# Another stored list of 102 shifts for the planner that orders an attention and feed-forward kernel

## The chip, the cores and the metric

The kernel runs on one core of a Trainium2 chip. The metric is device time in microseconds (us): the median of three runs of the kernel before is 573.95 us (573.7 to 574.1).

## What is computed

Local attention with a summary of the far keys, and behind it a feed-forward layer on the same tokens. Four batches, eight heads, 768 positions, 64 columns a head; the feed-forward layer has 3072 tokens, 512 columns and 2048 hidden units.

```python
k_sum = k.reshape(B, H, nb, block, D).max(axis=3)      # block 32, window 16
v_sum = v.reshape(B, H, nb, block, D).mean(axis=3)
scores_l = scale * np.matmul(q, k.transpose(0, 1, 3, 2))
mask_l = np.abs(pos[:, None] - pos[None, :]) < window
scores_s = scale * np.einsum('bhsd,bhnd->bhsn', q, k_sum) + np.log(block)
scores_all = np.concatenate([np.where(mask_l, scores_l, -1e9), scores_s], axis=-1)
a = softmax(scores_all)
x = np.matmul(a, np.concatenate([v, v_sum], axis=2))   # heads side by side: 3072 x 512
h = x @ w_in
g = h * (1.0 / (1.0 + np.exp(-h)))
out = g @ w_out
```

## The kernel before

The tokens are worked on in 12 chunks of 256 (chunk 0 to chunk 11). Each chunk needs the attention of two tiles of 128 positions, and then the feed-forward layer over 16 blocks of 128 hidden units, taken two at a time. The attention of later tiles is computed while the feed-forward layer of earlier chunks fills TensorE.

Chunk zero uses 32-bit matmuls (L915, L928) while the weights arrive. From chunk one on, weights and activations are split into a high and a low 16-bit half, and three products stand for one. Chunks one and two take the plain form (`job_f`: first matmuls L918, second matmuls L931); in the trace L918 runs from 85.0 to 173.8 us. From chunk three on (`FAST = 3`) the second matmul is done with seven products instead of eight (`job_fast`: L1006, L1046), which needs sums of the weights ("quads", made by `job_quad`: GpSimd at L986, VectorE at L991) and sums of the activations (GpSimd or VectorE at L1031).

The steps that the prediction speaks of, by line. ScalarE's L813 and VectorE's L814 read a finished attention tile out of a PSUM bank and write its high and its low half; the bank may take the next tile's L781 or L796 only when both are done. L871 makes the low half of a pair of weight blocks. L540 to L545 make the halves of q and k of a later tile, and L437 to L442 the scales of a batch. L505 and L507 are reductions over v, L411 one over k, and ScalarE's L413 and L431 take sums over k and q. Their inputs are loaded (L504, L410, L430, L539) into three staging buffers (`raw`), each of which has to be read before the next load into it starts. L1071 combines the four accumulator banks of a finished fast chunk into its output, which also frees those banks for the next chunk; L1129 does it for the end of the last chunk. L273 and L720, L722 belong to the softmax of batch zero, L944 and L947 to the activation of chunks zero to two.

The order is not written out by hand. Every step is an operation with a cost in ns on each engine that may do it, with its dependencies and a priority. `sweep` is a list scheduler: among the operations that are ready it takes the one that can start first, and among equals the one with the lower priority number, and it chooses the engine with it. `schedule` runs sweeps forward and backward for six rounds, keeps the best priorities, and then applies `MOVES`. Each entry of `MOVES` is (seed, start of a window, its length, size, block), in ns: `move` adds a random number of that size to the priority of the operations that the present order starts within the window, and sweeps again. The order after the last entry is the one that is issued, instruction by instruction, on every engine and on SyncE's DMA queue.

VectorE and GpSimd operations carry `port=("dve", "pool")` unless the call says otherwise, and the scheduler doesn't let two such operations run side by side.

```python
    def move(self, order, seed, at, span, size, block):
        rng, by = random.Random(seed), {}
        for i in sorted(o[2] for o in order if at <= o[0] < at + span):
            if i // block not in by:
                by[i // block] = rng.gauss(0, size)
            self.prio[i] += by[i // block]
        return self.sweep(self.prio, None, False)
```

Of the kernel before, what the change touches and what calls it, by code (L numbers as in the profile page):

```python
# [54 lines left out]
APART = 2  # L55
SOLO = [(0,), (1,)]
MOVES = (
# [26 lines left out]
)  # L84
NSUP = 2
FAST = 3
# [1210 lines left out]
```

## Time and profile before

| | us |
|---|---|
| median of three runs | 573.95 |
| the profiled execution | 573.44 |
| its span, first to last instruction | 571.7 |
| TensorE busy | 559.9 |
| VectorE busy | 482.2 |
| ScalarE busy | 388.0 |
| GpSimd busy | 195.8 |

Busy times are sums over the span. A "busy" TensorE is one with a matmul in its pipeline, whose end is modelled, so short pauses between matmuls don't show. DVE is VectorE, ACT ScalarE, POOL GpSimd, SP SyncE (which issues the DMAs), PE TensorE's matmuls and PEld its weight loads. L12 is line 12 of the kernel.

### The profile page before, as it was taken

The numbers are of one execution on the slowest core, as the hardware profiler recorded it, in microseconds if no ns is written. First come the engines' busy times: TensorE is split into PE (matmuls) and PEld (weight loads), VectorE is DVE, ScalarE is ACT, GpSimd is POOL, SyncE is SP. The second block draws the span as 40 slices with busy tenths as digits, with TensorE's granted clock in tenths as the row PEclk, the third lists the DMA queues.
The fourth block names the chain that finished last, engine by engine and source line by source line (L and its number), as shares of the span: only waits on it lengthen the run. The fifth ranks groups of instructions, "written<-read, shape, count | busy, mean of one in ns | idle before, by whom it ended". The sixth has DMA issues, their size and how long they took to land.

```text
span 571.7 us, 16049 instructions
## 1 busy us (share of the span) xinstructions
PE 559.9 (98%) x6426; PEld 455.6 (80%) x6426; DVE 482.2 (84%) x1159; ACT 388.0 (68%) x983; POOL 195.8 (34%) x292
## 2 busy tenths in 40 slices
PE   7999999989999999899999999999999999999996
PEld 3767657766666888788888888888888888888885
DVE  6999989989898886999988878998977978845655
ACT  4999989757867973667768865648767755533342
POOL 4302101561745542355433314252434333211110
PEclk9999999999999999999999999999999999999999
DMA  8999733333784679363673856544754239110101
GB/s 324 420 418 415 278 109 97 97 109 106 188 226 93 204 153 94 109 188 114 198 187 107 209 134 74 118 137 126 214 144 125 70 66 65 47 30 1 38 2 37
DMA packets 66737, 83.93 MB, mean 147 GB/s; under 512 B 44950, under 2 KB 45350, under 8 KB 64870
## 3 DMA queue, kind: packets, MB, share of 16 engines
q1 hardware_dynamic: 66662, 82.91, 52.4%
q8 instruction: 50, 0.82, 0.6%
q14 instruction: 25, 0.20, 0.1%
HBM read 61.60 MB, written 11.16 MB: 127 GB/s over the span
## 4 chain that ended last, share of the span: by engine, by line
PE 83%; DVE 7%; DMA 5%; ACT 3%; issue 1%; POOL 0%; SPq 0%; DVEq 0%; ACTq 0%
PE bank L1006 30%; PE bank L1046 25%; PE bank L931 6%; PE bank L918 6%; PE bank L915 5%; PE bank L928 4%; PE bank L796 2%; DVE wr L871 2%; PE bank L668 2%; DMA raw<-in_qF_dram 2%; DMA raw<-in_vR_dram 1%; PE bank L781 1%; DMA second<-in_qP_dram 1%; ACT e L707 1%; DMA raw<-in_qkT_dram 1%; DVE e L704 1%
## 5 line engine op out<-in xcount | busy, mean ns | idle before, releaser
L1006 PE MATMUL bank<-x,wr 128*128 128x256 f16 x1728 | 205.8, 273 | 0.0
L1031 POOL TENSOR_TENSOR wr<-wr 128x256 f32<-128x256 f32 (+1 forms) x172 | 122.5, 713 | 240.5 <-DVE wr L1022 127.4
L1006 PEld LDWEIGHTS <-wr 128*128 128x128 f16 x1728 | 167.8, 98 | 20.4
L1046 PE MATMUL bank<-wr 128*128 128x256 f16 x1491 | 179.9, 273 | 1.5 <-DVE raw L1071 1.5
L1046 PEld LDWEIGHTS <-wr 128*128 128x128 f16 x1491 | 144.6, 98 | 19.4 <-issue 1.7
L1021 ACT ACTIVATE wr<-bank,th 128x512 f32<-128x512 f32 x71 | 48.5, 683 | 54.2 <-PE bank L1006 53.9
L707 ACT ACTIVATE e<-e,mx 128x120 f32<-128x120 f32 x192 | 73.2, 383 | 8.1 <-DVE mx L704 8.0
L1022 DVE SCALAR_TENSOR_TENSOR wr<-wr,bank 128x512 f32<-128x512 f32 x71 | 48.5, 683 | 32.0 <-ACT wr L1021 31.7
L1033 ACT ACTIVATE wr<-wr 128x512 f16<-128x512 f32 x71 | 44.5, 626 | 35.4 <-POOL wr L1031 34.8
L1034 DVE SCALAR_TENSOR_TENSOR wr<-wr 128x512 f16<-128x512 f32 x71 | 49.7, 700 | 15.3 <-ACT wr L1033 15.1
L1026 ACT ACTIVATE wr<-wr 128x384 f16<-128x384 f32 x71 | 36.8, 519 | 36.8 <-DVE wr L1022 36.8
L1027 DVE SCALAR_TENSOR_TENSOR wr<-wr 128x384 f16<-128x384 f32 x71 | 45.5, 641 | 2.8 <-ACT wr L1026 2.6
L918 PE MATMUL bank<-x,wr 128*128 128x256 f16 x384 | 45.4, 273 | 0.0
L918 PEld LDWEIGHTS <-wr 128*128 128x128 f16 x384 | 37.2, 98 | 8.1 <-issue 0.6
L704 DVE CUSTOM_DVE_ANT_0 e<-bank,masks,qsc 128x120 f32<-128x120 f32 x144 | 41.7, 336 | 0.3 <-PE bank L668 0.3
L986 POOL TENSOR_TENSOR wr<-wr 128x256 f32<-128x256 f32 x32 | 30.9, 977 | 16.3 <-DVE wr L991 7.5
L707 ACT ACTIVATION_READ_ACCUMULATOR e<-e,mx 128x1 f32 x192 | 36.3, 189 | 0.0
L722 POOL TENSOR_SCALAR e<-e,sum 128x120 f32<-128x120 f32 x30 | 11.4, 395 | 65.3 <-DVE sum L715 31.7
L915 PEld LDWEIGHTS bank<-x,wr 128*128 128x128 f32 x144 | 24.8, 190 | 7.7 <-issue 4.2
L928 PE MATMUL bank<-wr,work 128*128 128x512 f32 x64 | 30.6, 596 | 0.0
L915 PE MATMUL bank<-x,wr 128*128 128x256 f32 (+1 forms) x144 | 30.6, 359 | 0.0
L760 DVE TENSOR_TENSOR first<-e,first 128x480 f16<-128x480 f32 x36 | 25.5, 714 | 0.1
(170 smaller groups left out, 788.4 us busy)
## 6 DMA issues: line engine op xcount, KB each, us to landing
wr<-in_w_dram SPq DMA_DIRECT2D x14, 1024.0 KB
raw<-in_qkT_dram SPq DMA_DIRECT2D x18, 576.0 KB
out_dram<-raw SPq DMA_DIRECT2D x23, 256.0 KB
first<-vd SPq DMA_DIRECT2D x30, 192.0 KB
raw<-in_kF_dram SPq DMA_DIRECT2D x12, 384.0 KB
raw<-in_qF_dram SPq DMA_DIRECT2D x9, 512.0 KB
raw<-in_vR_dram SPq DMA_DIRECT2D x12, 384.0 KB
raw<-in_vP_dram SPq DMA_DIRECT2D x9, 512.0 KB
```

Of the source, the lines that this page charges most:

```text
L704: plan.op({"dve": 262 if b else 206}, lambda e, i=i, j=j, et=et, mx=mx: nc.vector.tensor_tensor_reduce(out=et[:, i, :], in0=sc[j][:, i, :N ...
L707: plan.op({"act": 385}, lambda e, i=i, j=j, et=et, mx=mx: nc.scalar.activation(out=et[:, i, :], in_=et[:, i, :], func=AF.Exp, scale=-1.0, ...
L915: nc.tensor.matmul(out=o, lhsT=wi[:, ct * P:(ct + 1) * P], rhs=x0[:, ct, cs], start=(ct == 0), stop=(ct == NCT - 1))
L918: nc.tensor.matmul(out=o, lhsT=wip[:, part, ct * P:(ct + 1) * P], rhs=x[:, ct, :], start=(ct == 0 and q == 0), stop=(ct == NCT - 1 and q = ...
L928: nc.tensor.matmul(out=bank[ob[u]], lhsT=t[:, rows], rhs=wo, start=begins, stop=stops)
L1006: nc.tensor.matmul(out=h[:, at * CH:at * CH + CH], lhsT=wip[:, p, ct * P:(ct + 1) * P], rhs=x[:, ct, :], start=(ct == 0 and q == 0), stop= ...
L1021: plan.op({"act": 573}, lambda e: nc.scalar.activation(out=t, in_=h, func=AF.Tanh, scale=th[:, 0:1]), r=bk(k) + [("th", b % 2), "areas"], ...
L1022: plan.op({"dve": 604}, lambda e: nc.vector.scalar_tensor_tensor(out=t, in0=t, scalar=1.0, in1=h, op0=ALU.add, op1=ALU.mult), r=bk(k), w=t ...
L1027: plan.op({"dve": 470}, lambda e: nc.vector.scalar_tensor_tensor(out=ld, in0=src, scalar=SHRINK, in1=hd, op0=ALU.mult, op1=ALU.subtract), ...
L1031: plan.op({"pool": 135 + 290 * size, "dve": 213 if size == 1 else 459}, lambda e, o=o, x=x, y=y: eng[e].tensor_tensor(out=o, in0=x, in1=y, ...
L1034: plan.op({"dve": 610}, lambda e: nc.vector.scalar_tensor_tensor(out=ls, in0=sf, scalar=SHRINK, in1=hs, op0=ALU.mult, op1=ALU.subtract), r ...
L1046: nc.tensor.matmul(out=acc_of(c, m)[0], lhsT=x[:, left[m]], rhs=right[m](p), start=(opens and q == 0 and m in (1, 4, 2, 7)), stop=(closes ...
```

## The change

The tuple `MOVES` is replaced: 101 entries go and 102 come. The new list was chosen on a plan in which vector work takes longer in chunks one and two. Nothing else in the kernel changes: the costs, the dependencies, the rules of the scheduler and the list of operations are those of before.

```diff
 MOVES = (
-    (77065967, 539892, 8000, 2000, 1), (350253771, 327181, 20000, 200, 2), (631126651, 448333, 50000, 600, 1), (703916009, 173609, 8000, 2000, 1),
-    (908351244, 27961, 20000, 600, 2), (828492973, 176901, 20000, 200, 2), (387453712, 523354, 3000, 15000, 2), (975260573, 463713, 8000, 600, 1),
...
-    (720944112, 503864, 3000, 15000, 12),
+    (46148794, 194900, 8000, 6000, 2), (259609208, 234228, 3000, 600, 2), (429151876, 239758, 3000, 6000, 2), (548233728, 510331, 8000, 2000, 2),
+    (223928855, 486020, 50000, 600, 12), (821097478, 542829, 3000, 6000, 1), (942257997, 140504, 3000, 600, 12), (559197850, 325128, 3000, 15000, 1),
...
+    (674030052, 86227, 20000, 200, 1), (878329011, 29366, 20000, 200, 1),
 )
```

Sorted by the start of their windows, the old list has 5 entries that begin before 24 us, 20 from 24 to 86, 19 from 86 to 186, 8 from 186 to 240 and 49 after that; the new list has 3, 13, 17, 10 and 59.

## Rows read from the trace of the kernel before

**Rows 1.** The page: TensorE's busy time, and its granted clock in 40 slices.

```profile
PE 559.9 (98%) x6426; PEld 455.6 (80%) x6426; DVE 482.2 (84%) x1159; ACT 388.0 (68%) x983; POOL 195.8 (34%) x292
...
PEclk9999999999999999999999999999999999999999
```

**Rows 2.** Stretches: length; busy PE, PEld, DVE, ACT, POOL; clock, DMA share, GB/s.

```profile
0.00:25.00 25.00, 21.52 (x341) 13.00 (x342) 19.05 (x82) 16.95 (x61) 10.38 (x38) 1.00 0.94 364
...
80.00:100.00 20.00, 19.40 (x175) 12.79 (x174) 19.68 (x42) 19.38 (x40) 2.29 (x4) 1.00 0.25 74
100.00:120.00 20.00, 18.39 (x218) 13.16 (x217) 18.75 (x47) 13.98 (x39) 11.63 (x19) 1.00 0.27 71
120.00:186.00 66.00, 66.00 (x731) 44.99 (x728) 59.09 (x136) 48.20 (x116) 32.66 (x35) 1.00 0.60 157
...
230.00:240.00 10.00, 8.49 (x118) 7.33 (x116) 9.98 (x30) 7.22 (x26) 3.74 (x7) 1.00 0.19 62
240.00:545.00 305.00, 305.00 (x3784) 269.52 (x3783) 252.82 (x605) 193.23 (x505) 107.02 (x146) 1.00 0.47 114
545.00:571.70 26.70, 22.13 (x194) 18.74 (x192) 15.28 (x31) 8.56 (x16) 2.55 (x4) 1.00 0.06 21
```

**Rows 3.** Waits: engine, line <- releaser: us in total, times, longest.

```profile
DVE am L507 <- DMA raw<-in_vR_dram: 3.9, 2, 3.5
...
PE bank L781 <- DVE x L814: 1.6, 1, 1.6
PE bank L1046 <- DVE raw L1071: 1.5, 1, 1.5
...
PE bank L735 <- DVE third L273: 0.3, 1, 0.3
PE bank L931 <- DVE work L947: 0.3, 1, 0.3
```

**Rows 4.** Timeline of TensorE near 120 us: start, length, what, idle before.

```profile
119.71 1.15 PE L781 MATMUL bank<-third,v 120*64 120x64 f32 x32 [1.55 <-DVE x L814]
```

**Rows 5.** Timeline of VectorE, 110 to 120 us.

```profile
110.82 0.16 DVE L437 TENSOR_SCALAR qc<-qc 128x2 f32<-128x2 f32 x1
...
111.96 0.70 DVE L439 TENSOR_SCALAR qc<-qc 128x2 f32<-128x2 f32 x1
...
115.19 0.68 DVE L442 SCALAR_TENSOR_TENSOR qsc<-qsc 128x1 f32<-128x1 f32 x1
115.79 1.27 DVE L871 SCALAR_TENSOR_TENSOR wr<-wr,ws 128x1024 f16<-128x1024 f32 x1
116.99 0.74 DVE L542 SCALAR_TENSOR_TENSOR second<-raw,qsc,second 128x512 f16<-128x512 f32 x1
117.65 1.34 DVE L545 SCALAR_TENSOR_TENSOR second<-raw,qsc,second 128x640 f16<-128x640 f32 x1
118.91 0.74 DVE L814 SCALAR_TENSOR_TENSOR x<-bank,vsc,x 128x512 f16<-128x512 f32 x1
```

**Rows 6.** Timeline of ScalarE, 115 to 117 us.

```profile
115.49 0.69 ACT L813 ACTIVATE x<-bank,vsc 128x512 f16<-128x512 f32 x1
```

**Rows 7.** Timeline of GpSimd, 108 to 124 us.

```profile
111.90 0.73 POOL L986 TENSOR_TENSOR wr<-wr 128x256 f32<-128x256 f32 x1
...
117.14 3.12 POOL L986 TENSOR_TENSOR wr<-wr 128x256 f32<-128x256 f32 x3 [1.29 <-DVE wr L871]
```

**Rows 8.** Lines L986 and L545: ns min/median/max, first and last start in us.

```profile
L986 POOL TENSOR_TENSOR wr<-wr x32: 720/894/1786, 111.9 to 186.5; 128x256 f32<-128x256 f32 x32
...
L545 DVE SCALAR_TENSOR_TENSOR second<-raw,qsc,second x18: 869/884/1344, 117.6 to 459.1; 128x640 f16<-128x640 f32 x18
```

**Rows 9.** The chain of work that ended last, in order of time: start, us, what.

```profile
94.71 0.85 DVE am L507
...
218.33 7.22 DMA raw<-in_vR_dram
...
234.42 0.74 DVE raw L1071
```

46 rows, old and new, of the table MOVES are left out of this document.

## The prediction

> **What bounds the kernel now.** I read the page's engine table first, then busy time by stretch, then what TensorE waited for, and last the lines around its two long waits. TensorE is busy 559.9 of 571.7 us at a granted clock of 0.9 or more of full speed in every slice, 1.00 by stretch, the upper of its two levels (2.4 GHz) [rows 1, 2]. So the end is set by TensorE's work plus the moments in which it has none, and a change of order can win only those moments. The stretches show where they lie: 3.48 us before 25 us, 0.60 between 80 and 100, 1.61 between 100 and 120, 1.51 between 230 and 240, 4.57 after 545, and none in the other stretches [rows 2]. (Ends of matmuls are modelled, so these are lower bounds, good enough to place the waits.) The table of waits names the middle ones: 1.6 us for VectorE's L814, 1.5 us for VectorE's L1071, and 0.3 twice for L273 and L947 [rows 3]. All four wait for VectorE, and three of the four lie in the stretches from 80 to 120 us, in chunk one; the wait for L1071 belongs to the end of chunk three.
>
> The longest wait in detail: TensorE's L781 starts at 119.71 after 1.55 us of idleness [rows 4], because it overwrites the bank that L814 still reads. L814's other input, ScalarE's L813, ended at 115.49 + 0.69 = 116.18 [rows 6]. But L814 started only at 118.91: ahead of it in VectorE's queue stood L871 (115.79), L542 (116.99) and L545 (117.65) [rows 5]. And the vector work there is longer than elsewhere: L439 on two columns takes 0.70 us where its neighbour L437 of the same shape takes 0.16, L442 takes 0.68, and L545 takes 1.34 where its median is 0.884 [rows 5, 8]. The same moments hold GpSimd's L986: 0.73 us from 111.90, and three of them in 3.12 us from 117.14 [rows 7]. L439 ended at 112.66, L986 at 112.63. The excess of the three vector instructions is (0.70 - 0.16) + (0.68 - 0.16, L437 standing for its base) + (1.34 - 0.88) = 1.52 us, as long as the wait itself.
>
> **The change part by part.** Nothing computed is added or removed: 101 stored shifts go, 102 come, and every cost, rule and dependency of the planner stays. What moves is the order of instructions on each engine and, with it, on SyncE's DMA queue; any operation that has more than one engine to choose from may change engine too. The new order isn't in the trace of before, so its terms are read as idle time that can go or come.
>
> *The wait for L814.* A list that was kept because it does well when vector work is slow in chunks one and two has a reason to put L814, which TensorE needs at once, ahead of L542 and L545, which serve scores of a later tile. The price of that order can be read: in L542's place, right behind L871, it would start at 116.99 instead of 118.91, 1.92 us earlier, more than the 1.55 to be won [rows 4, 5]. Value taken: -1.55 us. Bounds: 0, if another vector step takes L814's place in front of TensorE, and -1.55 - 2 x 0.3 = -2.15, if the two short waits of the same chunk [rows 3] go with it. I take the value between, because the two short waits hang on a stretch where VectorE is busy 19.68 of 20 us [rows 2] and there is no room to go ahead in.
>
> *The wait for L1071.* It is outside the two chunks. VectorE sat idle for 3.5 us until a load of vR had landed, 7.22 us after its issue at 218.33, and L1071 was reached at 234.42 after the burst that had piled up [rows 3, 9]. A longer booking of vector work two chunks earlier neither brings this load forward nor empties the three staging buffers. Value taken: 0. Bounds: -1.51 (the whole idle time of that stretch [rows 2]) and, above, the price worked out for the slower rival, below.
>
> *The rest of chunks three to eleven.* TensorE has no idle time from 240 to 545 us while VectorE is busy 252.8 of 305 us [rows 2]: shifts there are covered by 52 us of vector slack. Value 0; where that cover is locally gone the cost is one vector step, 0.74 us for an L1071 [rows 9], and nothing is to be gained.
>
> *Start and end.* Of the shifts whose window begins before 24 us the old list has five and the new three, so the first loads may come in another order. TensorE's idle time bounds the gain, 3.48 us at the start and 4.57 us at the end [rows 2]; the nearest row for a loss is one load landing late, up to 7.22 us [rows 9]. I take 0 for both, since idle time there follows from the first loads and the last store, which no order of vector work removes.
>
> The profiled execution took 573.44 us. Sum: 573.44 - 1.55 + 0 + 0 + 0 = 571.89. The median of the runs, 573.95, stands 0.51 above it, so on the median's scale: **572.4 us**.
>
> *A rule weighed.* The coincidence of L986 with the stretched vector steps [rows 5, 7] has a rule beside it. The Trainium skill, page "SBUF — State Buffer", section "SBUF: two separate sides", says that VectorE and GpSimd share one pair of ports as an exclusive lock: whoever starts first keeps it for the whole instruction and the other stands still. The trace agrees with it in L439, which ends within 0.03 us of L986. By the rule the collisions don't vanish in another order, which speaks against the change and is the second rival below; by the forecast's sum 571.89 stands, by the rule alone 573.44.
>
> **The rivals.**
> 1. *The wait moves but stays as long.* GpSimd's 32 quad steps of L986 still run between about 112 and 187 us at a median of 0.894 us [rows 8], and VectorE is already busy 18.75 + 59.09 of the 86 us from 100 to 186 [rows 2]. Only 8.2 us are free for whatever the collisions cost, 1.52 us for three of them. Another order lets them fall on other vector steps, and if one of those feeds TensorE, 1.5 us come back there: 573.95 us. The same time results if the change doesn't do what it says: the planner that replays the shifts keeps its old costs, so the windows may catch other operations than those they were chosen on. For it: the shifts' costs and rules are untouched, and TensorE's waits come from coincidences of this size. Against it: in 120 to 186 us the same L986 cost TensorE nothing [rows 2].
> 2. *Both waits go.* Any other order around 218 to 234 may issue the load of vR earlier. Then 573.95 - 1.55 - 1.51 = 570.9 us. For it: the wait for L1071 hangs on a single late load. Against: nothing in the change aims there.
> 3. *Slower: vector work put off from chunks one and two lands in front of L1071.* Booked longer, the reductions that can wait (L507 at 94.71, for instance, 0.85 us of the chain in chunk one [rows 9]) are pushed later, to where they stand with their loads between 190 and 238 us. There TensorE already waits, so there is no cover left. One more load of vR with its two reductions in front of L1071 costs 2 x 0.85 = 1.7 us if it has landed, and 7.22 + 1.7 - 3.5 = 5.4 us if it has not, the 3.5 being the idle time that exists anyway [rows 3, 9]. Middle 3.6. With the gain in chunk one kept that is 573.95 - 1.55 + 3.6 = 576.0 us. It decides from 1.55 + 1.15 = 2.7 us of added delay, so from about 2.7 - 1.7 = 1.0 us of waiting for a load that is not there in time.
>
> **How the numbers follow.** A measurement of this kernel can tell about 0.2%, 1.15 us, from no change; the line for faster is 572.80, that for slower 575.10. Forecast 572.4: 0.34. Rival 2, 570.9: 0.12. Rival 1, 573.95: 0.29. Rival 3, 576.0: 0.25. The forecast lies 0.4 us beyond the line, so 0.03 of it is counted as no change: faster 0.31 + 0.12 = 0.43, same 0.29 + 0.03 = 0.32, slower 0.25. The range reaches from just below rival 2 (570.9 less part of the two short waits) to rival 3: 570.7 to 576.2; what is left out is the upper half of rival 3 and a little below rival 2, about 0.17 together. The likeliest case's own range is 571.7 to 573.0.
>
> **What would show it.** Right: TensorE's waits no longer name L814, the stretch from 100 to 120 has it busy nearly throughout, L814 starts within a microsecond of L813's end, and a wait for L1071 of about 1.5 us stands near 235. Wrong by rival 1: TensorE's waits in 85 to 186 us still add up to about 2 us under another VectorE line, with L986 beside it. By rival 2: no wait over 0.5 us between 25 and 545. By rival 3: a wait of 3 us or more between 190 and 280 that ends on VectorE, with a DMA into the staging buffers behind it. A first matmul on real data later or earlier by over a microsecond would upset the term taken as 0 at the start.

## The result and the profile after

The changed kernel takes 579.51 us (median of four runs, 577.29 to 581.02) against 573.83 us for the kernel before in the same comparison. The ratio is 1.0096, interval 1.0081 to 1.0111: **slower by about 1%**, where 572.4 us and a gain were forecast. The profiled execution is the longest of the four runs, 581.02 us with a span of 579.3, so the trace below shows 7.6 us more span than that of before, while the medians differ by 5.7. Its granted clock is 0.993 over the span; the shortest run's is 1.000.

Stretches of the changed kernel, columns as in [rows 2]:

```profile
0.00:25.00 25.00, 20.90 (x319) 11.43 (x321) 17.22 (x77) 15.24 (x53) 10.44 (x38) 0.93 0.95 364
80.00:100.00 20.00, 19.74 (x175) 13.87 (x174) 19.93 (x39) 19.64 (x40) 2.42 (x7) 1.00 0.23 67
100.00:120.00 20.00, 19.76 (x216) 13.67 (x214) 18.06 (x45) 15.68 (x44) 8.85 (x16) 1.00 0.32 96
120.00:186.00 66.00, 65.59 (x710) 44.18 (x712) 59.76 (x128) 49.91 (x122) 29.99 (x35) 1.00 0.60 156
230.00:240.00 10.00, 6.92 (x102) 5.78 (x100) 10.00 (x36) 7.11 (x24) 3.72 (x7) 1.00 0.37 73
240.00:545.00 305.00, 301.93 (x3736) 265.68 (x3736) 249.18 (x593) 189.42 (x495) 111.86 (x159) 0.99 0.49 116
```

Against [rows 2]: from 100 to 120 us TensorE is now busy 19.76 us where it was 18.39; from 230 to 240 it is busy 6.92 where it was 8.49; and the long stretch from 240 to 545, which had no idle time, has 3.07 us of it. What it waited for, and VectorE's wait for vR (columns as in [rows 3]):

```profile
PE bank L1046 <- ACT e L720: 2.4, 1, 2.4
...
PE bank L1046 <- DVE raw L1071: 1.8, 2, 1.2
...
PE bank L1046 <- ACT wr L1075: 1.3, 1, 1.3
PE bank L781 <- DVE x L814: 0.7, 2, 0.4
PE bank L1006 <- DVE wr L1022: 0.7, 1, 0.7
...
DVE am L507 <- DMA raw<-in_vR_dram: 10.9, 2, 6.2
```

The wait for L814, 1.6 us in one piece before, is 0.7 in two pieces: 0.41 at the same place, and a new one of 0.27 at 63.6 us, in chunk zero. But L1046 now waits 2.4, 1.8 and 1.3 us, and VectorE waits for vR 10.9 us in two pieces where it was 3.9 [rows 3].

Matmuls of the two traces can be paired by line and number, since TensorE runs the same ones in each stage. The distance between a matmul of after and its partner says where time went. Where both orders run a stage alike, it is +2.86 us on the last matmul of chunk zero (L928, 84.6 us in before), +1.53 from the middle of L918 on, +4.98 from 239 to 348 us, +8.41 from 405 us to the last L1046, and +7.61 at the end. (Matmuls that change places with others lie off these values.) So the start costs 2.86, chunk one gives back 1.33, two places cost 3.45 and 3.43, and the end gives back 0.80; together 7.61.

**The two places.** The timeline of TensorE in the changed kernel (start, length, what, idle before), only the instructions that waited there:

```profile
236.93 0.49 PE L1046 MATMUL bank<-wr 128*128 128x256 f16 x3 [1.32 <-ACT wr L1075]
237.95 0.81 PE L1046 MATMUL bank<-wr 128*128 128x256 f16 x6 [0.54 <-DVE raw L1071]
239.99 1.24 PE L1046 MATMUL bank<-wr 128*128 128x256 f16 x6 [1.22 <-DVE raw L1071]
...
363.27 2.78 PE L1006 MATMUL bank<-x,wr 128*128 128x256 f16 x24 [0.67 <-DVE wr L1022]
370.78 0.49 PE L1046 MATMUL bank<-wr 128*128 128x256 f16 x3 [2.40 <-ACT e L720]
```

The waits at L1046 come some 9 and 10 us after VectorE, which works in order, had stood still, each time at the first reduction of a load of vR:

```profile
228.13 0.95 DVE L507 TENSOR_REDUCE am<-raw 128x1 f32<-128x768 f32 x1 [4.67 <-DMA raw<-in_vR_dram]
...
360.81 0.95 DVE L507 TENSOR_REDUCE am<-raw 128x1 f32<-128x768 f32 x1 [6.24 <-DMA raw<-in_vR_dram]
```

The load itself, in the chain of waits of the changed kernel (start, us), takes longer than the 7.22 us of [rows 9]:

```profile
218.43 9.68 DMA raw<-in_vR_dram
...
351.20 9.58 DMA raw<-in_vR_dram
```

What was issued ahead of it stands in SyncE's queue (start, length, line). First the changed kernel:

```profile
217.66 0.66 SPq L637 DMA_DIRECT2D first<-vd  x2
218.43 0.47 SPq L504 DMA_DIRECT2D raw<-in_vR_dram  x1
...
350.43 0.66 SPq L637 DMA_DIRECT2D first<-vd  x2
351.20 0.55 SPq L504 DMA_DIRECT2D raw<-in_vR_dram  x1
```

The same two places in the kernel before:

```profile
214.81 1.21 SPq L637 DMA_DIRECT2D first<-vd  x2
218.33 0.36 SPq L504 DMA_DIRECT2D raw<-in_vR_dram  x1
...
345.83 0.33 SPq L504 DMA_DIRECT2D raw<-in_vR_dram  x1
346.76 0.67 SPq L637 DMA_DIRECT2D first<-vd  x2
```

L637 loads the attention's values of a tile, two loads of rows of 2 KB. For the last tile of a batch the second has only 79 rows (158 KB; the first has 96). Before, L637 stood 3.5 us ahead of vR at the first place and behind it at the second. In the new order it stands right ahead of vR at both, 0.8 us. (The last tile of the third batch, at 473 us before and 483 us after, has no load of vR behind it.) What happens then is in the DMA view of the changed kernel from 350 to 361 us (40 slices of 0.275 us):

```profile
GB/s 0 0 0 0 0 209 223 238 112 67 86 235 354 369 212 86 22 30 62 205 222 72 39 39 31 22 30 22 30 22 22 30 22 34 22 22 34 10 82 289
...
first<-vd SPq DMA_DIRECT2D x1, 192.0 KB
first<-vd SPq DMA_DIRECT2D x1, 158.0 KB
```

After the bursts the queue moves 22 to 39 GB/s for some 4 us, and only then the last burst comes. The DMA records of the trace, counted by packet size per us, say what these are:

```
us after the first issue        0   1   2   3   4   5   6   7   8   9
after, from 350.4: 2 KB (L637)  2  94   9   9  12  13  12  13  11   0
                   3 KB (vR)    0   2  40  78   0   0   0   0   1   7
```

The 96 rows of L637 are through in two us. The 79 others go at 9 to 13 per us, 84 ns each (the median of a packet) and 80 ns from one start to the next, which is one at a time. Of the 128 rows of vR, 120 go past them within four us; the last eight, one sixteenth, start only when the 79 have ended. This agrees with the Trainium skill, page "DMA: Bandwidth & Descriptors", section "Why a DMA increments its semaphore by 16 and not by 1": a load is spread over the largest number of DMA engines, up to 16, that divides its rows. By that rule 96 and 128 rows go to 16 engines, and 79, a prime, to one; the eight late rows of vR are that engine's share.

### The profile page after: what moved, and what is told of

It is laid out like the page before. It is cut to its first block, busy times and chain, and to the rows that moved or that the text cites. A ratio compares the mean times of both kernels' runs of the same rounds, so it can differ in the third digit from the quotient of the medians.

```text
span 579.3 us, 16077 instructions
## 1 busy us (share of the span) xinstructions
PE 564.1 (97%) x6427; PEld 457.3 (79%) x6427; DVE 478.1 (83%) x1147; ACT 391.4 (68%) x994; POOL 193.5 (33%) x302
## 4 chain that ended last, share of the span: by engine, by line
PE 72%; ACT 10%; DVE 8%; DMA 7%; issue 1%; POOL 1%; SPq 0%; DVEq 0%; ACTq 0%; POOLq 0%
PE bank L1006 28%; PE bank L1046 23%; PE bank L931 6%; PE bank L918 5%; DMA raw<-in_vR_dram 3%; DVE wr L871 2%; ACT e L707 2%; ACT wr L843 2%; PE bank L796 2%; PE bank L668 2%; DMA raw<-in_qF_dram 2%; PE bank L928 1%; ACT wr L839 1%; DMA second<-in_qP_dram 1%; PE bank L915 1%
## 5 line engine op out<-in xcount | busy, mean ns | idle before, releaser
L1031 POOL TENSOR_TENSOR wr<-wr 128x128 f32<-128x128 f32 (+1 forms) x180 | 122.1, 678 | 226.2 <-DVE wr L1022 110.7
L1046 PE MATMUL bank<-wr 128*128 128x256 f16 x1491 | 182.6, 273 | 5.5 <-ACT e L720 2.4
L1046 PEld LDWEIGHTS <-wr 128*128 128x128 f16 x1491 | 144.4, 98 | 24.3 <-issue 4.4
L918 PE MATMUL bank<-x,wr 128*128 128x256 f16 x384 | 45.0, 273 | 0.0
L918 PEld LDWEIGHTS <-wr 128*128 128x128 f16 x384 | 37.3, 98 | 8.2 <-issue 0.6
L986 POOL TENSOR_TENSOR wr<-wr 128x256 f32<-128x256 f32 x32 | 27.9, 883 | 29.2 <-ACT second L540 7.8
L722 POOL TENSOR_SCALAR e<-e,sum 128x120 f32<-128x120 f32 x32 | 11.8, 385 | 74.6 <-DVE sum L714 30.6
L928 PE MATMUL bank<-wr,work 128*128 128x512 f32 x64 | 29.9, 594 | 0.0
L760 DVE TENSOR_TENSOR first<-e,first 128x480 f16<-128x480 f32 x36 | 27.5, 764 | 0.1
## 6 DMA issues: line engine op xcount, KB each, us to landing
raw<-in_qkT_dram SPq DMA_DIRECT2D x18, 576.0 KB
```

Of the source, the lines that this page charges most:

```text
L918: nc.tensor.matmul(out=o, lhsT=wip[:, part, ct * P:(ct + 1) * P], rhs=x[:, ct, :], start=(ct == 0 and q == 0), stop=(ct == NCT - 1 and q = ...
L1031: plan.op({"pool": 135 + 290 * size, "dve": 213 if size == 1 else 459}, lambda e, o=o, x=x, y=y: eng[e].tensor_tensor(out=o, in0=x, in1=y, ...
L1046: nc.tensor.matmul(out=acc_of(c, m)[0], lhsT=x[:, left[m]], rhs=right[m](p), start=(opens and q == 0 and m in (1, 4, 2, 7)), stop=(closes ...
```

## The experiments

Theory: L637's 79 rows, issued right ahead of vR, hold vR back; VectorE waits in order, works off a burst, and L1071, L1076 and the steps for L1046 come late. The rivals were work put off onto VectorE (the prediction's rival 3 as it was put) and, for the rest, the start. Lines of the experiments lie 3 or 7 further down than those of before where code was added (L1046 is then L1049 or L1053; L507 stays or is L514). Orders were changed by taking operation `a` out of the planned order and issuing it right ahead of operation `b`.

**e1, the 79 rows cut into 64 and 15, order of the changed kernel.**

```diff
-                nc.sync.dma_start(out=vv[at:at + hi - lo, z], in_=vd_t[b - 1][lo:hi])
+                cut = lo + HALF if hi - lo == NKEY - NB - HALO - 2 else hi
+                for x, y in ((lo, cut), (cut, hi)):
+                    if x < y:
+                        nc.sync.dma_start(out=vv[at + x - lo:at + y - lo, z], in_=vd_t[b - 1][x:y])
```

> The changed kernel, with the load of 79 rows at L637 issued as two loads of 64 and 15 rows. Theory A (a late load): those 79 packets of 2 KB run one after the other on one DMA engine (79 x 84 ns = 6.6 us), the load of vR issued right behind them (218.43 and 351.20) lands only after 9.7 and 9.6 us, VectorE stands 4.67 and 6.24 us at L507, and TensorE's waits near 236 and 368 us are the result. Then VectorE's waits for vR fall under 1.5 us each, TensorE's waits there under 1 us, and the time falls by 4 to 6 us, to about 574. Theory B (too much vector work put off into chunk three): VectorE is busy without a gap from 230 to 240 whatever lands when; TensorE's waits stay over 2 us at both places and the time falls by less than 1.5 us.

Measured: 571.46 us, ratio to before 0.996 (0.9948 to 0.9972). VectorE's waits for vR fall to 1.5 us together and TensorE has no wait at L1049 (L1046) at all; its stretches have it busy throughout at both places:

```profile
230.00:240.00 10.00, 10.00 (x133) 8.85 (x131) 9.57 (x18) 8.38 (x26) 4.79 (x7) 1.00 0.39 119
340.00:380.00 40.00, 40.00 (x527) 35.22 (x525) 36.65 (x87) 28.58 (x79) 17.80 (x26) 1.00 0.51 147
```

One cut load turns the changed kernel from 5.7 us slower into 2.3 us faster. That is 8.0 us, more than the 4 to 6 expected: besides the losses of 3.45 and 3.43 us, the wait that the kernel before has at the first place goes too (the paired matmuls go from +1.09 to -0.58 there).

**e2, vR issued ahead of L637, no load cut.**

```diff
+AHEAD_OF = [(1221, 1060), (1889, 1728)]
```

> The changed kernel with one order undone: at two places the load of vR (L504) is issued ahead of the pair of loads at L637 instead of right behind it, as the kernel before has it at the second of the two places. No transfer is altered. Theory A (queue order behind a slow load): as good as splitting, 4 to 6 us less, about 574, and the chain shows landings of vR of 3 to 4 us. Theory B (vector work put off): no change, 578 to 580.

Measured: 571.82 us, 0.9969 (0.9958 to 0.9981). The order of the two issues alone gives nearly the same as the cut. A wait for the next load of vR, 3.5 us, remains near 354, and costs TensorE 1.1 us (L1053 on L1083, which are L1046 on L1076).

**e4, the other way round: the kernel before, with L637 ahead of vR at 346 us.**

```diff
+AHEAD_OF = [(1728, 1889)]
```

> The kernel before with the harm put in at one place: the pair of loads at L637 near 346.5 us is issued ahead of the load of vR at 345.8 instead of behind it, as the changed kernel has it. Theory A: VectorE waits 4 to 7 us for vR near 350 to 357, TensorE waits 2 to 3.5 us after it, and the time is 576 to 577.5. Theory B (the order of these loads doesn't matter): 573.95, no new wait of TensorE over 0.5 us.

Measured: 582.11 us, 1.0149 (1.0125 to 1.0173). One swap in the old order costs 8 us; in its profiled execution (580.11, the shortest of five) the paired matmuls go from -0.46 to +6.68 at that place. The direction is as the theory has it, the size is larger. Its trace, VectorE's timeline and TensorE's wait:

```profile
356.64 0.95 DVE L514 TENSOR_REDUCE am<-raw 128x1 f32<-128x768 f32 x1 [7.21 <-DMA raw<-in_vR_dram]
...
PE bank L1053 <- ACT wr L1033: 4.6, 1, 4.6
```

and its stretches, where the granted clock, which falls during the wait, shows the rest (76 matmuls in the 8 us at 1.00, 48 in the 8 us at 0.70; a figure between 0.50 and 1.00 is a mean over the two levels, 1.2 and 2.4 GHz):

```profile
356.00:360.00 4.00, 0.00 (x0) 0.00 (x0) 3.36 (x6) 0.28 (x1) 0.24 (x1) 0.75 0.13 28
360.00:368.00 8.00, 7.30 (x48) 5.46 (x49) 7.02 (x24) 5.11 (x17) 3.90 (x6) 0.70 0.44 102
368.00:376.00 8.00, 8.00 (x76) 7.18 (x74) 8.00 (x21) 4.88 (x15) 2.62 (x4) 1.00 0.26 73
```

**e9 and e10, is it the prime number of rows or the size?** The changed kernel with the 79 rows cut into 78 and 1, and into 61 (again a prime) and 18.

```diff
-                cut = lo + HALF if hi - lo == NKEY - NB - HALO - 2 else hi
+                cut = lo + 78 if hi - lo == NKEY - NB - HALO - 2 else hi
```

(e10 has `lo + 61`.)

> The changed kernel with the 79-row load cut into 78 and 1 rows (e1 cut it into 64 and 15). Theory: the 79 rows crawl because 79 is a prime, so that the rows can't be shared out and one DMA engine works them one after another; 78 rows have divisors and one row is one packet, so the crawl goes and the kernel takes 571 to 572.5 us, as the 64 and 15 rows did; VectorE's waits for vR at L507 stay under 1.5 us each. Rival: what helped in e1 was the smaller load (64 rows of 2 KB) or the second queue entry as such; then 78 rows crawl like 79 and the kernel stays at 577 to 581 us with a wait for vR of over 4 us.

> The changed kernel with the 79-row load cut into 61 and 18 rows. Theory: 61 is a prime, so 61 packets still go one after another at the 84 ns of the changed kernel's packets, 5.1 us instead of 6.6; vR lands about 1.5 us earlier than in the changed kernel, and the two waits of VectorE at L507 shrink by about 1.5 us each (from 4.7 and 6.2 to about 3 and 4.7). What the end gains is at least that less where the wait is covered: 574 to 578 us, between the changed kernel and e1. Rival (size or number of loads counts, not divisors): 61 rows are a smaller load than the 64 of e1, so the time is that of e1, 571 to 572.5 us, and no wait for vR is over 1.5 us.

Measured: e9 571.2 us, 0.9963 (0.9951 to 0.9976); e10 575.22 us, 1.0029 (1.0017 to 1.0041). VectorE at the two places, first e9, then e10:

```profile
222.13 0.95 DVE L507 TENSOR_REDUCE am<-raw 128x1 f32<-128x768 f32 x1
...
348.57 0.95 DVE L507 TENSOR_REDUCE am<-raw 128x1 f32<-128x768 f32 x1 [0.45 <-DMA raw<-in_vR_dram]
```

```profile
225.28 0.95 DVE L507 TENSOR_REDUCE am<-raw 128x1 f32<-128x768 f32 x1 [3.08 <-DMA raw<-in_vR_dram]
...
355.03 0.95 DVE L507 TENSOR_REDUCE am<-raw 128x1 f32<-128x768 f32 x1 [4.99 <-DMA raw<-in_vR_dram]
```

78 rows are as good as 64, so it wasn't the smaller size that helped in e1. In e10 there is a second load too, and the smaller load of 61 rows crawls again, at 84 ns a packet in the records; so it wasn't the second load either. The two waits are shorter by 1.59 and 1.25 us (from 4.67 and 6.24), where 18 rows of 84 ns make 1.51. That settles the cause of the two stalls: a number of rows that can't be shared out, and a wanted load right behind it.

**e5 and e6, the kernel before with one thing mended each; e7 with both.** e5 has e1's cut. e6 puts L542 and L545 behind L814 (both are issued right ahead of operation 753, which comes after L814): the first step of the prediction, done by itself.

```diff
+AHEAD_OF = [(566, 753), (568, 753)]
```

> The kernel before with the load of 79 rows at L637 issued as loads of 64 and 15 rows. Theory A (a load on one DMA engine delays vR): VectorE's wait of 3.5 us at L507 near 222 and TensorE's wait of 1.5 us for L1071 near 236 go, the time is 572.2 to 572.8, and the wait of 1.6 us for L814 stays. Theory B (the wait for L1071 is VectorE's own burst of work): no change, 573.7.

> The kernel before with one order of VectorE altered: L542 and L545 near 117 us are issued behind L814 instead of ahead of it. It tests the first term of the prediction, -1.55 us, alone. Theory: TensorE's wait of 1.6 us for L814 goes and the time is 572.2 to 572.6. Rival (the wait moves, because the lengthened vector instructions fall on the next step): 573.4 to 574.

> Both of these edits in the kernel before. Theory: the two waits are independent, TensorE has no wait over 0.5 us between 25 and 545 us, and the gains add up to 2.5 to 3.0 us: 570.8 to 571.3. Rival: TensorE, ahead by 1.5 us, meets the next late step and the sum is under 2 us.

Measured: e5 572.62 us, 0.9975 (0.9965 to 0.9985); e6 572.94, 0.9985 (0.9976 to 0.9994); e7 571.31, 0.9958 (0.9944 to 0.9971). In e5 the wait for L1071 is gone (TensorE busy 10.00 us from 230 to 240 where it was 8.49) and that for L814 stands at 1.6. So the 79 rows were behind the wait for L1071 in the kernel before as well. In e6 it is the other way round: busy 19.95 of 20 from 100 to 120 us, and L1053 (L1046) still waits 1.2 for L1078 (L1071). e6 gains 0.94 us, between what its theory (1.3 to 1.7) and its rival expected, e5 gains 1.26, and e7 gains 2.57, no less than the sum of 2.20: the two waits are independent.

**e3 and e8, the start.** e3 is the changed kernel with two early score operations moved forward and their filling matmuls with them. e8 has the order of before for everything planned before 30 us, then that of after, and e1's cut.

```diff
+AHEAD_OF = [(37, 19), (84, 19)]
+FILLS = {37: 11, 19: 0}
```

```diff
+        start = sorted(o for o in start if o[0] < CUT)    # CUT = 30000
+        done = {o[2] for o in start}
+        return start + sorted(o for o in best if o[2] not in done)
```

> The changed kernel with the start of the kernel before: TensorE does the scores of the second tile (L671, L675, second half) and the filling matmuls ahead of the first sums at L579, instead of behind them. Theory: in the changed order the sums wait at the head of TensorE's queue for the load of vP (12.88 us), and the scores start at 13.88 instead of 11.09; undone, the chunk-zero matmuls start 2.0 to 2.8 us earlier and the time falls by as much, to about 577. Rival: the start is set by the loads and by a lower granted clock in the first 25 us, so the order gives back less than 1 us.

> The order of the kernel before for everything that it starts before 30 us, then the changed kernel's order, with the 79-row load split. The changed order lost 2.3 us in the first 25 us of its split version too. Theory: that is the order of the first steps, and 571.46 falls by 2 to 2.5 us, to 569 to 569.5, with the first matmul of L915 at 22.6 to 23 us. Rival: the start is late for reasons that lie in single executions (a load that lands later, a lower granted clock), and the time stays within 1 us of 571.5.

Measured: e3 581.43 us, 1.0133 (1.0112 to 1.0153), no better than the changed kernel: the second tile's scores start at 11.21 us as intended, but the paired matmuls still lie 2.5 us late at the end of chunk zero, with a new wait of 1.5 us at L742 for GpSimd's L729 (L735 for L722). e8 572.89, 0.9982 (0.997 to 0.9994), and not the 571.46 of e1: up to 25 us TensorE is busy 22.06 us, but from 25 to 80 only 53.29 of 55, and the matmuls lie 2.7 us late at the end of chunk zero, probably because the first steps of one order are followed by an order that counted on other ones; that was not tested. Neither shows what the start costs by itself.

What the start consists of can be read from two executions with the same early order. TensorE's timeline of the changed kernel, then that of e2 (lines 7 further down):

```profile
7.54 0.40 PE L671 MATMUL bank<-first,second 64*64 64x96 f32 x8 [1.96 <-DMA second<-in_qP_dram]
...
9.33 3.62 PE L367 MATMUL bank<-ident 128*128 128x512 bf16 x11
12.88 1.06 PE L579 MATMUL bank<-wr,sums 128*32 128x512 f32 x8
13.88 0.40 PE L671 MATMUL bank<-first,second 64*64 64x96 f32 x8
```

```profile
6.95 0.40 PE L678 MATMUL bank<-first,second 64*64 64x96 f32 x8 [0.65 <-DMA second<-in_qP_dram]
...
8.20 2.55 PE L374 MATMUL bank<-ident 128*128 128x512 bf16 x11
10.68 1.06 PE L586 MATMUL bank<-wr,sums 128*32 128x512 f32 x8
11.67 0.40 PE L678 MATMUL bank<-first,second 64*64 64x96 f32 x8
```

In the kernel before, the second tile's scores start at 11.09. The new order puts eight L579 ahead of them, which is 1.0 us in both. The rest, 2.21 us between the two, is the landing of the first load (0.59) and the clock: the eleven filling matmuls take 3.62 us in the one and 2.55 in the other, and the granted clock from 8 to 12 us is 0.57 in the one and 1.00 in the other. At the end of chunk zero the paired matmuls lie 0.95 (e2), 1.52 (e9), 1.59 (e10), 2.41 (e1) and 2.86 us (the changed kernel) behind those of before. So the order's own part is about a microsecond by the least of these (an estimate), and the rest differs from one execution to the next. What decides it was not found; in e1 the first scores take 0.60 us instead of 0.40 although the granted clock shows no fall there.

## Why the prediction was wrong

**The step that failed** is the value 0 for the rest of chunks three to eleven, together with the 0 for L1071. The prediction said that shifts there "are covered by 52 us of vector slack" and that "where that cover is locally gone the cost is one vector step, 0.74 us". The slack is a sum over 305 us and can't be drawn on ahead of time: VectorE works in order, so the 6.24 us for which it stood at L507 delayed everything behind it in its queue, and the work piled up behind it comes as a burst ahead of the step for which TensorE waits. Measured: +3.45 and +3.43 us in the changed kernel, +7.14 for the one swap of e4. e1, e2, e9 and e10 alter nothing but this load or its place in the queue, and the losses go, or shrink as the load does.

**What was not looked at** is SyncE's queue. The prediction said that the order on the DMA queue moves, read that one load of vR took 7.22 us [rows 9], and did not ask why it did, nor what stood ahead of it. Its neighbour, L637 at 214.81, was in the trace, and so was the next place, where vR came first and VectorE's L507 (349.81) had no wait. e5 shows that this row was the mechanism already at work. The planner books L637's pair at 1050 ns and knows nothing of what it does to a load behind it; both stored lists are equally blind to it, and the old one met it once, the new one twice.

**Point by point.**
- The wait for L814, -1.55: near in size, but not by the way described, so part of this hit is luck. Chunk one gives back 1.33 us, and the wait itself is 0.41 where it was 1.55. But the new order doesn't put L814 ahead of L542 and L545. VectorE of the changed kernel still runs both ahead of it (L545 at 116.25), with ScalarE's L813 at the end:

```profile
117.51 1.22 DVE L542 SCALAR_TENSOR_TENSOR second<-raw,qsc,second 128x512 f16<-128x512 f32 x1
118.65 1.27 DVE L871 SCALAR_TENSOR_TENSOR wr<-wr,ws 128x1024 f16<-128x1024 f32 x1
...
120.45 0.74 DVE L814 SCALAR_TENSOR_TENSOR x<-bank,vsc,x 128x512 f16<-128x512 f32 x1
...
118.17 0.69 ACT L813 ACTIVATE x<-bank,vsc 128x512 f16<-128x512 f32 x1 [2.06 <-PE bank L781]
```

  L814 starts 1.59 us after L813's end, not within the microsecond that the prediction gave as its sign. What changed is when L545 and L542 come: both had started before L813 did, so less stood between. L814 starts 2.28 us after L813's start instead of 3.42 [rows 5, 6], and these 1.14 us are those by which the wait is shorter; TensorE does the same twelve L918 and six L931 in between. The order that the prediction described is e6, worth 0.94 by itself.
- The wait for L1071, 0, said to be untouched: wrong. The idle time from 230 to 240 us grew from 1.51 to 3.08, and the clock fell behind it. Stretches of the changed kernel:

```profile
236.00:240.00 4.00, 1.32 (x10) 0.88 (x10) 4.00 (x8) 4.00 (x12) 2.07 (x4) 1.00 0.14 14
240.00:244.00 4.00, 4.00 (x22) 2.94 (x22) 3.59 (x6) 1.87 (x7) 2.48 (x3) 0.57 0.70 267
244.00:250.00 6.00, 6.00 (x57) 5.39 (x56) 5.01 (x8) 3.97 (x7) 3.10 (x6) 1.00 0.52 157
...
371.00:376.00 5.00, 5.00 (x87) 4.37 (x85) 5.00 (x10) 5.00 (x11) 2.52 (x4) 1.00 0.33 125
```

  TensorE, busy 1.32 us of the four from 236 to 240, then works at a clock of 0.57: 22 matmuls in 4 us, where at 1.00 it does 57 in 6, or 38 in 4. That is 16 matmuls, 1.7 us at 9.5 per us. Idle 1.57 more and 1.7 of clock make 3.3 of the 3.45. At the second place 2.40 us of idleness in one piece were followed by a clock of 1.00, and the loss of 3.43 is the idle time of 3.07 and a rest of 0.36 that stays open. That the clock stayed up there belongs to this execution: in e3, which has the same wait of 2.40 us at the same place, it fell:

```profile
371.00:376.00 5.00, 4.52 (x66) 3.24 (x66) 4.95 (x12) 5.00 (x11) 3.14 (x5) 0.66 0.36 121
```

- Start and end, 0 for both: wrong by +2.86 and -0.80 in this execution. The reason given, that idle time there follows from the first loads and the last store, left out that an order can put other matmuls ahead of the scores on TensorE (1.0 us of L579), and what the clock adds.
- Rival 3 had the direction, its first place (between 190 and 280 us, VectorE behind a DMA into a staging buffer) and 576.0 us, against 577.3 to 581.0 measured. Its mechanism was not the right one. e2 keeps the new list and with it all the work on VectorE, moves two loads, and is at 571.82: not work that was put off, but a load held up in the queue. Its price for a load that isn't there, 5.4 us for one place, is of the size that one place can cost (e4: 7.14), but it stood at a middle of 3.6, and a second place was not thought of.
- The rule that the prediction weighed belongs to its rival 1, not to the second as it says. The Trainium skill (page "SBUF — State Buffer", section "SBUF: two separate sides") also limits the lock, on VectorE's side, to instructions in a two-port mode or with two inputs in SBUF; the prediction leaves that out, and no run here tells these apart. The lengthened vector steps did not go: L542 takes 1.22 us in the lines above, and L545, behind L814 in e6, still 1.35. They cost TensorE less: the stretches from 100 to 186 us lose 0.65 us where they lost 1.61 [rows 2].

**What stays open**: what sets the start, and when the clock falls. The runs of the changed kernel spread over 3.7 us, and their mean granted clocks are 0.993, 0.994, 0.997 and 1.000 for 581.02, 579.37, 579.65 and 577.29 us; 0.007 of 579 us is 4 us. In the profiled run the clock falls at the start (8 to 12 us) and behind the first stall (240 to 244). e1, e9 and e10, with the same start, spread over 1.5 us at most; so the spread goes mainly with the clock, and e3 and e4, which keep a stall, spread as far (3.5 and 4.9). Even the run at 1.000 is over 3 us slower than the kernel before. With the 79 rows cut, the new list (e1 571.46, e9 571.20) is about 1 us ahead of the old one (e5 572.62), near the limit of what the runs tell apart and close to what the forecast's first term promised; e7, the old list with L814 ahead as well, is level with it (571.31).

## What to carry to other kernels

Before a change of order is costed, read the DMA queue of the old trace like an engine: what stands ahead of each load that an in-order engine waits for, and how long from issue to landing. A row such as 7.22 us for a load whose rows are through in three us elsewhere (in the kernel before, from 345.8 us on) is a fault to explain, not a constant to reuse. Slack summed over a long stretch covers no stall of an in-order engine; and a load whose number of rows is a prime, 79 here, is worth one more instruction to cut it. When a forecast term comes out near its size, look in the new trace whether it came by the way described.

## What was not expected of the hardware

- A load of 79 rows of 2 KB takes over 6 us, at 9 to 13 packets per us and 84 ns each, where 96 rows are through in two, and a load of 128 rows issued behind it has 120 rows in place within four us and the last eight only when the 79 are done. With 78 rows and 1, VectorE's wait for that load is 0.5 us at most; with 61 it is shorter by 1.25 and 1.59 us.
- A stall of 4.6 us of TensorE was followed by 8 us at a mean granted clock of 0.70 (e4), and one stretch of 4 us with 1.32 us of work by 4 us at 0.57. A stall of 2.40 us was followed by 5 us at 1.00 in the changed kernel and by 5 us at a mean of 0.66 in e3.
